# Attention with two exponential paths: VectorE's exp in half-step exponent bits, read through four shifted copies

## The chip, the core and the metric

The program runs on one NeuronCore of one Trainium2 chip. The metric is the time of one execution on the device in microseconds. The engines are TensorE (PE in the profile), VectorE (DVE), ScalarE (ACT), GpSimd (POOL) and SyncE (SP, which issues DMAs). PE writes into PSUM; ACT and DVE read PSUM; POOL works on SBUF alone.

## What is computed

One transformer block, conditioned by a vector c (adaptive layer norm), on 2048 tokens of width 512, in bfloat16:

```python
mod = (_silu(c) @ w_mod).reshape(c.shape[0], 6, 1, -1)
sa, ca, ga, sb, cb, gb = ...
h = _layernorm(x) * (1 + ca) + sa
qkv = (h @ wqkv)                        # 32 heads of 16
scores = einsum('bhqd,bhkd->bhqk', q, k) * 16 ** -0.5
o = einsum('bhqk,bhkd->bhqd', softmax(scores), v)
x = x + ga * (o @ wo)
h = _layernorm(x) * (1 + cb) + sb
x = x + gb * (gelu(h @ w1 + b1) @ w2 + b2)      # 512 -> 1376 -> 512
```

The bulk is the exponential: 32 heads x 2048 queries x 2048 keys.

## The kernel before

**Tiles.** Scores are computed transposed, with 128 keys on the partitions and 512 queries along the free dimension. The work is cut into 32 runs. A run handles one block of 512 queries for four heads at once (or, for the last block, 256 queries for eight heads) against 16 key tiles of 128 keys. A key tile of a run has four score blocks of 128x512, one for each of four row groups of PE. That makes 32 x 16 x 4 = 2048 score blocks. Each is one matmul at L852 (function `qk`), with the 16-wide heads selected by zeros in the masked q.

**Two paths to exp.** On path A the score blocks go in groups of three and two into PSUM tiles `st`, and ACT computes exp into `pt` (L925). On path D each block goes into a PSUM bank `ax`, and DVE computes exp by writing bits (L966): q is scaled so that a score is in 1/128 of a power of two, DVE adds a bias and writes int16, and these bits, read as bfloat16, are 2 to that power with a mantissa that is linear between powers of two. The error of the linear mantissa is averaged out: the same bits shifted by 26, 51, 77 and 102 (fifths of an octave, L987, 2048 columns at a time, into `sh`) are further copies, and each copy is multiplied with a copy of V that is scaled by the inverse power (`PH_W`), so that the five products add up to an exponential with a smaller ripple. The first copy is `ph` itself with the unscaled V (`VEB`); the others use `VX`. The last copy of some tiles is made by POOL in four pieces of 512 columns (`by_pool`, L1002, into `sg`).

**PV.** For each copy, four matmuls at L1037 (`pv_op`) add one key tile's product with V to the run's accumulator `od` in PSUM, whose 17th column for each head is the softmax denominator. A key tile of path A has one such PV group, a key tile of path D five. Tiles 2, 5, 8, 11 and 14 (`DKS`) of each run may take path D; ACT takes the ones that D has not reached when its own are finished (`next_tile`).

**The order of the work.** [...] A planner (`Plan`) has a list of ready operations for each engine with a duration, a priority, the buffers that they need and the time at which those come free. At each step it commits the operation that can start first; among those that can start within a short time of each other it takes the lowest value of priority plus a pseudorandom amount (`spread`, up to 0.15), which is drawn from a seed. `SEEDS` has 32 seeds, one for each 25 us of planned time. Matmuls of zeros into the running accumulator (`zeros`, L478 and L1028) and of a zero tile (`warm`, L462) are put into PE's pauses when the planner counts too little PE work in the last microseconds.

**Around the attention.** In the first 30 us the input is normalised, modulated and projected; POOL fills the copies `VX` (memsets at L583, scaling at L787). Denominators go out and back through DRAM (`normalise`). The output projection and the MLP of a finished query block (`block_tail`; L1204, L1270, L1210) run between the runs of the next one. After the last run only the last 256 queries' share remains (`last_half`; L1350, L1381, L1210).

**Buffers of path D.** `ph` has four buffers, `sh` three, `sg` one, all of 2048 int16 columns. A `ph` buffer comes free when all its readers are done: the PV group that reads it and the shifts.

Of the kernel before, what the change touches and what calls it, by code (L numbers as in the profile page):

```python
# [12 lines left out]
ALU = mybir.AluOpType  # L13
# [9 lines left out]

NPH = 5
PH_SH = [round(128 * j / NPH) for j in range(NPH)]


def _bf16(v):  # L30
    m, e = math.frexp(v)
    return math.ldexp(round(m * 256) / 256, e)


PH_W = [_bf16(2.0 ** (-sh / 128)) for sh in PH_SH]


def _gain():
    tot = 0.0
    for f in range(128):  # L40
        for sh, w in zip(PH_SH, PH_W):
            n, m = divmod(f + sh, 128)
            tot += w * 2.0 ** n * (1 + m / 128) / 2.0 ** (f / 128)
    return tot / 128


PH_B = 127.0 * 128.0 - 128.0 * math.log2(_gain())

# [10 lines left out]
FILL = 2.1  # L63
HOLD = 0.0
SPREAD = 0.15
SEEDS = (911, 176, 171, 436, 700, 513, 198, 752, 533, 913, 224, 342, 292, 722, 961, 407, 718, 35, 564, 862, 16, 658, 167, 214, 547, 531, 221, 674, 720, 595, 429, 662)
HEAT = 1.7


# [40 lines left out]
class Plan:  # L110
# [59 lines left out]
    def spread(self, o):  # L170
        x = ((sum(map(ord, o.kind)) if o.eng == "PE" else o.fn.__code__.co_firstlineno if o.fn else 0) * 2654435761 ^ SEEDS[min(int(self.now // 25.0), len(SEEDS) - 1)] * 2246822519) & 0xFFFFFFFF
        x = ((x ^ x >> 15) * 2246822519) & 0xFFFFFFFF
        return SPREAD * ((x ^ x >> 13) & 1023) / 1024.0
# [107 lines left out]
def kernel(  # L281
# [14 lines left out]
    nc = tc.nc  # L296
# [11 lines left out]
    FL = F - (NF - 1) * P  # L308
    VW = 17
    EPS = 1e-5  # L310
    QSC = 0.25 * 128.0 / math.log(2.0)
    ESC = math.log(2.0) / 128.0
    DKS = (2, 5, 8, 11, 14)
    NPT = 4
    FEW = 1
# [160 lines left out]
    def zeros(r):  # L476
        for i in range(4):
# [27 lines left out]
    VX = {(t, ph): keep.tile([P, 32 * VW + 15], BF16, name=f"VX{t}_{ph}")  # L505
          for t in DKS for ph in range(1, NPH)}
    kT = [[keep.tile([P, QB], BF16, name=f"kT{cc}_{b}") for b in range(NQ)] for cc in range(NC)]
# [26 lines left out]
    first = {}  # L534
# [53 lines left out]
    for b in range(NQ):  # L588
        late = (lambda: True) if b == 0 else (lambda: first_ln[0])
        o_v0[b] = v_init(VEB[b], PH_W[0], 1.0 + b, late)  # L590
        for t in DKS:
            if t // TPB == b:
                o_vx0[t] = [x for ph in range(1, NPH) for x in v_init(
                    VX[(t, ph)].unsqueeze(1), PH_W[ph], 1.5 + b, lambda: first_ln[0])]

# [172 lines left out]
    def make_v(b, cc, kind, acq, eng, after=None):  # L768
# [14 lines left out]
        for t in DKS:  # L783
            if t // TPB == b:
                def scale(o, t=t):
                    for ph in range(1, NPH):
                        nc.gpsimd.tensor_scalar(  # L787
                            out=v_cols(VX[(t, ph)])[:, 8 * cc:8 * cc + 8, 0:16],
                            in0=v_cols(v_tile(t, 0))[:, 8 * cc:8 * cc + 8, 0:16], scalar1=PH_W[ph],
                            scalar2=0.0, op0=ALU.mult, op1=ALU.add)  # L790
# [40 lines left out]
    def next_tile(which, r):  # L831
        while r < NR:
            if which == "A" and own[r]:
                return r, own[r].pop(0)
            if which == "A" and shared[r]:
                left[r] -= NPH - 1
                return r, shared[r].pop()
# [99 lines left out]
    def qk_d():  # L937
        r, kt, rows = at["D"]
        if not rows:
            got = next_tile("D", r)  # L940
            if got is None:
                return
            r, kt = got
            rows = [0, 1, 2, 3]
            at["D"][:] = r, kt, rows
            o_ph[0] = op("NIL", None, 0.0, (), lat=0.0, prio=0.0, acq=r_ph)
            d_e[:] = []
        ph = o_ph[0]
        live["D"] += 1
        deps, qm = qk_deps(r, kt)  # L950
        last = len(rows) == 1

        def go(o):
            n_d[0] += 1
            rows.remove(o.row)
            qk(o, 0, r, kt, o.row)
            live["D"] -= 1
        o = op("PE", go, MM, deps + [ph], lat=PEL, mode=("qk", rows[0]), kind="qkD", acq=r_ax, rel=(qm,),
               gate=lambda: n_d[0] - n_d[1] < 2)
        o.rows = rows  # L960

        def ex(e):
            n_d[1] += 1
            units[0] += 1
            d_last[0] = True
            nc.vector.tensor_scalar(out=ph.tile[:, o.row * QB:(o.row + 1) * QB], in0=o.tile, scalar1=PH_B,  # L966
                                    scalar2=0.0, op0=ALU.add, op1=ALU.max)
        d_e.append(op("DVE", ex, 0.6, (o,), lat=DL, prio=0.5, rel=(o,)))
        d_e[-1].run, d_e[-1].qk = r, o
        if last:  # L970
            shifts(r, kt, ph, list(d_e))
# [4 lines left out]
    def shifts(r, kt, first, es):  # L976
        def parts(o):
            return lambda: [o.tile[:, h * QB:(h + 1) * QB].bitcast(BF16) for h in range(4)]
        pv_op(r, kt, 0, es, parts(first), (first,))
        for j in range(1, NPH):  # L980
            if j == NPH - 1 and g_left[0] <= G_MAX and plan.now > G_FROM and (
                    r > a_run[0] or len(own[r]) + len(shared[r]) >= G_TILES):
                by_pool(r, kt, j, first, es, parts)
                continue
            def shift(o, j=j):
                d_last[0] = False
                nc.vector.tensor_scalar(out=o.tile, in0=first.tile, scalar1=PH_SH[j], scalar2=None, op0=ALU.add)  # L987
            sh = op("DVE", shift, 0.6, es, lat=DL, prio=2.0, acq=r_sh, rel=(first,), port=True)
            sh.run, sh.alt = r, True
            pv_op(r, kt, j, (sh,), parts(sh), (sh,))  # L990
# [4 lines left out]
    def by_pool(r, kt, j, first, es, parts):  # L995
        sh = op("NIL", None, 0.0, es[:1], lat=0.0, prio=0.0, acq=r_sg)
        got = []
        for h in range(4):
            def go(o, e=es[h]):
                g_left[0] -= 1  # L1000
                c = slice(e.qk.row * QB, (e.qk.row + 1) * QB)
                after_dve(nc.gpsimd.tensor_scalar(  # L1002
                    out=sh.tile[:, c], in0=first.tile[:, c], scalar1=1.0, scalar2=float(PH_SH[j]),
                    op0=ALU.mult, op1=ALU.add))
            g_left[0] += 1
            got.append(op("POOL", go, G_US, (sh, es[h]), lat=0.1, prio=G_PRIO, kind="beside", rel=(first,), port=True,
                          gate=lambda: plan.beside(G_MIN)))
        pv_op(r, kt, j, got, parts(sh), (sh,))

    def pv_op(r, kt, ph, deps, srcs, owners):  # L1010
        cc, par, hb = run_heads(r)

        def go(o):
            if not begun[r]:
                begun[r] = True
                pv_run[0] = r
                o_od[r] = o
                r_od.free[0] = 1e18
                o.acq, o.slot = r_od, 0
                o.tile = r_od.alloc(0)  # L1020
                first = True
            else:
                first = False
            left[r] -= 1
            got = srcs()
            if first and hb is not None:
                for i in range(4):
                    nc.tensor.matmul(out=o_od[r].tile[32 * i:32 * i + 32, :], lhsT=warm[:, 0:32],  # L1028
                                     rhs=warm[:, 0:1].to_broadcast([P, QB]), start=True,
                                     stop=False, tile_position=(0, 32 * i))  # L1030
            parts = (par,) if hb is None else (0, 1)
            for n, p in enumerate(parts):
                for i in range(4):
                    c0 = VW * (8 * cc + 2 * i + p)
                    w = QB if hb is None else HB
                    at = n * HB
                    nc.tensor.matmul(out=o_od[r].tile[32 * i:32 * i + 32, n * HB:n * HB + w],  # L1037
                                     lhsT=v_tile(kt, ph)[:, c0:c0 + 32],
                                     rhs=got[i][:, at:at + w], start=first and hb is None,
                                     stop=(left[r] == 0 and p == parts[-1]), tile_position=(0, 32 * i))  # L1040
            if o.extra:
                zeros(r)
            if left[r] == 0:
                o_last[r] = o
                ended.append(r)
        left[r] += 0

        def gate():
            return begun[r] or r_od.free[0] <= plan.now + 0.05 and (r == 0 or left[r - 1] == 0)
        o = Op("PE", go, 0.2225, list(deps) + o_v[(cc, kt // TPB)], lat=PEL, mode=("pv", 0), kind="pv",  # L1050
               rel=owners, gate=gate)
        o.last_left = lambda: left[r]
        plan.add(o)
# [396 lines left out]
    while True:  # L1450
# [7 lines left out]
        while ended:  # L1458
            r = ended.pop(0)
# [80 lines left out]
```

## Time and profile before

| | |
|---|---|
| time, three runs | 779.01 us median (778.93 to 780.66) |
| span of the profiled execution, first to last instruction | 777.3 us |
| PE busy | 736.9 us (95%) |
| DVE busy | 710.6 us (91%) |
| ACT busy | 750.7 us (97%) |
| POOL busy | 323.5 us (42%) |
| ACT's exp, L925 | 626 instructions, 709.7 us |
| DVE's exp, L966 | 484 instructions, 317.5 us |
| DVE's shifts, L987 | 406 instructions, 276.6 us |
| POOL's shift pieces, L1002 | 312 instructions, 191.3 us |

A row of a group gives line, engine, operation, output and inputs with shapes, then the count; behind the first bar the busy time in us (overlaps counted once in the page's groups) and the mean duration in ns; behind the second the idle time of the engine just before these instructions and what ended most of it. A row of a stretch gives its length, then for each engine busy time and the number of instructions, then the granted clock of PE, the share of time in which the DMA engines were busy, and GB/s. A row of the timeline or of the chain of waits gives start and duration in us. A PE that is busy isn't PE at its peak: matmuls overlap, and their ends are modelled.

### The profile page before, as it was taken

The numbers are of one execution on the slowest core, as the hardware profiler recorded it, in microseconds if no ns is written. First come the engines' busy times: TensorE is split into PE (matmuls) and PEld (weight loads), VectorE is DVE, ScalarE is ACT, GpSimd is POOL, SyncE is SP. The second block draws the span as 40 slices with busy tenths as digits, with TensorE's granted clock in tenths as the row PEclk, the third lists the DMA queues.
The fourth block names the chain that finished last, engine by engine and source line by source line (L and its number), as shares of the span: only waits on it lengthen the run. The fifth ranks groups of instructions, "written<-read, shape, count | busy, mean of one in ns | idle before, by whom it ended". The sixth has DMA issues, their size and how long they took to land.

```text
span 777.3 us, 21242 instructions
## 1 busy us (share of the span) xinstructions
PE 736.9 (95%) x8476; PEld 273.7 (35%) x8476; DVE 710.6 (91%) x1226; ACT 750.7 (97%) x677; POOL 323.5 (42%) x619
## 2 busy tenths in 40 slices
PE   8999999999998999999999999999999999999998
PEld 3433333233322222223323233233334444434455
DVE  6888699899999999999999899999899999998983
ACT  4999999999999999999999999999999999999993
POOL 6534645434445345545323144343334543252231
PEclk9999999999999999999999999999999999999999
DMA  7124010000210001001100100001020101010000
GB/s 217 35 76 143 19 40 28 26 12 12 76 26 23 19 18 50 19 7 27 40 20 21 35 19 26 12 21 33 29 56 22 25 19 45 16 26 18 26 18 28
DMA packets 38549, 27.74 MB, mean 36 GB/s; under 512 B 17941, under 2 KB 33846, under 8 KB 38450
## 3 DMA queue, kind: packets, MB, share of 16 engines
q1 hardware_dynamic: 38442, 26.39, 12.3%
q8 instruction: 66, 1.08, 0.6%
q14 instruction: 33, 0.27, 0.1%
q10 hardware_dynamic: 8, 0.00, 0.0%
HBM read 20.77 MB, written 2.61 MB: 30 GB/s over the span
## 4 chain that ended last, share of the span: by engine, by line
ACT 42%; PE 29%; DVE 15%; issue 11%; DMA 2%; POOL 0%; SPq 0%; DVEq 0%; ACTq 0%
ACT pt L925 41%; PE od L1037 9%; PE st L852 8%; DVE ph L966 5%; DVE sh L987 5%; PE ax L1210 3%; PE ax L852 2%; PE ax L1270 2%; PE ax L732 1%; DVE ln_s L637 1%; DVE OD L1062 1%; DMA blk<-in_w_mod_dram 1%; DMA dc<-dn 1%; PE ax L1204 1%; DVE z L648 1%
## 5 line engine op out<-in xcount | busy, mean ns | idle before, releaser
L925 ACT ACTIVATE pt<-st 128x1536 bf16<-128x1536 f32 x626 | 709.7, 1367 | 2.5 <-PE st L852 1.3
L966 DVE TENSOR_SCALAR ph<-ax 128x512 int16<-128x512 f32 x484 | 317.5, 681 | 26.9 <-PE ax L852 24.5
L1002 POOL TENSOR_SCALAR sg<-ph 128x512 int16<-128x512 int16 x312 | 191.3, 622 | 259.6 <-DVE sh L987 159.2
L987 DVE TENSOR_SCALAR sh<-ph 128x2048 int16<-128x2048 int16 x406 | 276.6, 709 | 4.9 <-PE od L1037 3.6
L852 PE MATMUL st<-qm,kT 32*128 32x512 bf16 x1564 | 245.2, 382 | 23.1 <-ACT pt L925 18.1
L852 PE MATMUL ax<-qm,kT 32*128 32x512 bf16 x484 | 166.6, 379 | 2.1 <-DVE ph L966 1.3
L852 PEld LDWEIGHTS <-kT 32*128 32x128 bf16 x2048 | 83.1, 91 | 239.1 <-issue 229.3
L1037 PE MATMUL od<-sh,VX 128*32 128x512 bf16 (+1 forms) x2036 | 144.1, 340 | 2.3 <-DVE sh L987 2.1
L1037 PE MATMUL od<-pt,VEB 128*32 128x512 bf16 (+1 forms) x1952 | 142.9, 340 | 0.9 <-DVE OD L1062 0.5
L1037 PEld LDWEIGHTS <-VEB 128*32 128x32 bf16 x2560 | 60.7, 96 | 74.2 <-issue 60.9
L1037 PEld LDWEIGHTS <-VX 128*32 128x32 bf16 x2432 | 57.7, 95 | 79.3 <-issue 68.3
L1089 POOL TENSOR_TENSOR OT<-OD,RB 128x256 bf16<-128x256 f32 x38 | 27.5, 736 | 64.7 <-DVE sh L987 57.7
L1037 PE MATMUL od<-ph,VEB 128*32 128x512 bf16 (+1 forms) x608 | 47.9, 340 | 1.2 <-DVE OD L1062 1.1
L1270 PE MATMUL ax<-blk,W 128*128 128x512 bf16 (+1 forms) x176 | 44.1, 356 | 0.1
L787 POOL TENSOR_SCALAR VX<-VEB 128x128 bf16<-128x128 bf16 x80 | 27.2, 342 | 31.5 <-DVE VEB L663 26.8
L732 PE MATMUL ax<-blk,w 128*128 128x512 bf16 x124 | 36.2, 383 | 1.3 <-DMA w<-in_A_wqkv_dram 0.8
L1210 PE MATMUL ax<-w,g 128*128 128x512 bf16 x128 | 33.7, 381 | 1.1 <-ACT g L1280 0.6
L1089 POOL TENSOR_TENSOR OS<-OD,RB 128x256 bf16<-128x256 f32 x24 | 17.5, 742 | 40.1 <-DVE sh L987 39.8
L1037 PE MATMUL od<-sg,VX 128*32 128x512 bf16 (+1 forms) x396 | 31.3, 339 | 0.0
L1275 DVE TENSOR_SCALAR g<-ax,b1c 128x512 bf16<-128x512 f32 (+1 forms) x44 | 29.3, 676 | 1.3 <-PE ax L1270 1.1
L478 PE MATMUL od<-warm 128*32 128x512 bf16 x268 | 26.0, 382 | 0.0
L637 DVE BATCH_NORM_STATS2 ln_s<-xb 128x6 f32<-128x512 bf16 x32 | 21.6, 675 | 1.5 <-DMA xb<-in_A_x_dram 1.4
(108 smaller groups left out, 409.6 us busy)
## 6 DMA issues: line engine op xcount, KB each, us to landing
RB<-rn SPq DMA_DIRECT2D x124, 64.0 KB
xb<-in_A_x_dram SPq DMA_DIRECT2D x7, 512.0 KB
out_dram<-o SPq DMA_DIRECT2D x16, 128.0 KB
qm<-qs SPq DMA_DIRECT2D x120, 16.0 KB
W<-in_B_w_dram SPq DMA_DIRECT2D x1, 1376.0 KB
w<-in_A_wqkv_dram SPq DMA_DIRECT2D x3, 384.0 KB
blk<-in_w_mod_dram SPq DMA_DIRECT2D x2, 512.0 KB
xb<-in_w_mod_dram SPq DMA_DIRECT2D x2, 512.0 KB
```

Of the source, the lines that this page charges most:

```text
L637: nc.vector.bn_stats(out=st6, in_=src)
L732: return chain([(lambda ps, j=j: nc.tensor.matmul(out=ps[:, 0:QB], lhsT=w.tile[:, j, cc * P:(cc + 1) * P], rhs=o_h[b].tile[:, j, :], start ...
L852: nc.tensor.matmul(out=o.tile[:, k * QB:(k + 1) * QB], lhsT=kT[cc][kb][rows, ko * P:(ko + 1) * P], rhs=qm.tile[rows, par, :] if hb is None ...
L925: nc.scalar.activation(out=e.tile[:, 0:total * QB], in_=o.tile[:, 0:total * QB], func=ACT.Exp, scale=ESC)
L966: nc.vector.tensor_scalar(out=ph.tile[:, o.row * QB:(o.row + 1) * QB], in0=o.tile, scalar1=PH_B, scalar2=0.0, op0=ALU.add, op1=ALU.max)
L987: nc.vector.tensor_scalar(out=o.tile, in0=first.tile, scalar1=PH_SH[j], scalar2=None, op0=ALU.add)
L1002: after_dve(nc.gpsimd.tensor_scalar(out=sh.tile[:, c], in0=first.tile[:, c], scalar1=1.0, scalar2=float(PH_SH[j]), op0=ALU.mult, op1=ALU.add))
L1037: nc.tensor.matmul(out=o_od[r].tile[32 * i:32 * i + 32, n * HB:n * HB + w], lhsT=v_tile(kt, ph)[:, c0:c0 + 32], rhs=got[i][:, at:at + w], ...
L1089: two = beside(lambda c: nc.gpsimd.tensor_tensor(out=OT.tile[:, c], in0=OD.tile[:, c], in1=o5.tile[:, c], op=ALU.mult), (OT,), (OD, o5), f ...
L1210: nc.tensor.matmul(out=ps, lhsT=g[:, f, col:col + P], rhs=rhs, start=(f == 0), stop=(f == NF - 1))
L1270: mm = chain([(lambda ps, f=f, j=j, f0=f0: nc.tensor.matmul(out=ps[:, (f - f0) * N:(f - f0 + 1) * N], lhsT=W1[:, j, f * P:(f + 1) * P], rh ...
L1275: ev.append(op("DVE", lambda o, f=f, f0=f0, mm=mm: nc.vector.tensor_scalar(out=g.tile[:, f, 0:N], in0=mm.tile[:, (f - f0) * N:(f - f0 + 1) ...
```

## The change

VectorE's exp writes its result in half steps: q is scaled by twice as much (`QSC` with `FINE` = 2), so the int16 counts 1/256 of an octave, and the exponent bias of 127 x 128 is no longer in it. These numbers aren't bfloat16 bits themselves, so the direct reading of `ph` is dropped. Four copies (0, 1/4, 1/2, 3/4 of an octave) are all made by an instruction with two operations: times 0.5, plus the bias, the shift and a fraction of 0.25 or 0.75, rounded when written as int16. The first copy goes with `VEB`, the other three with `VX`, of which there are now three for each of five tiles instead of four. ACT's exp has half the scale. The copy made by POOL is now the fourth one (j = 3), with a factor of 0.5 where 1.0 stood. The 32 seeds are other numbers. No other line differs; `Plan`, its durations and priorities, and the buffers are the same.

```diff
-NPH = 5
-PH_SH = [round(128 * j / NPH) for j in range(NPH)]
+NPH = 4
+FINE = 2
+PH_SH = [128 * j / NPH + 0.25 + 0.5 * (j % 2) for j in range(NPH)]
...
-PH_W = [_bf16(2.0 ** (-sh / 128)) for sh in PH_SH]
+PH_W = [_bf16(2.0 ** (-j / NPH)) for j in range(NPH)]
...
-PH_B = 127.0 * 128.0 - 128.0 * math.log2(_gain())
+PH_0 = 127.0 * 128.0
+PH_B = -FINE * 128.0 * math.log2(_gain())
+PH_LOW = -FINE * PH_0
...
-SEEDS = (911, 176, 171, 436, 700, 513, 198, 752, 533, 913, 224, 342, 292, 722, 961, 407, 718, 35, 564, 862, 16, 658, 167, 214, 547, 531, 221, 674, 720, 595, 429, 662)
+SEEDS = (133, 8, 244, 706, 635, 613, 830, 607, 557, 981, 249, 97, 553, 633, 53, 586, 376, 469, 873, 940, 563, 742, 976, 448, 82, 180, 131, 20, 555, 353, 321, 992)
...
-    QSC = 0.25 * 128.0 / math.log(2.0)
-    ESC = math.log(2.0) / 128.0
+    QSC = 0.25 * 128.0 * FINE / math.log(2.0)
+    ESC = math.log(2.0) / (128.0 * FINE)
...
             nc.vector.tensor_scalar(out=ph.tile[:, o.row * QB:(o.row + 1) * QB], in0=o.tile, scalar1=PH_B,
-                                    scalar2=0.0, op0=ALU.add, op1=ALU.max)
+                                    scalar2=PH_LOW, op0=ALU.add, op1=ALU.max)
...
-        pv_op(r, kt, 0, es, parts(first), (first,))
-        for j in range(1, NPH):
+        for j in range(NPH):
...
-                nc.vector.tensor_scalar(out=o.tile, in0=first.tile, scalar1=PH_SH[j], scalar2=None, op0=ALU.add)
+                nc.vector.tensor_scalar(out=o.tile, in0=first.tile, scalar1=1.0 / FINE, scalar2=PH_0 + PH_SH[j],
+                                        op0=ALU.mult, op1=ALU.add)
...
                 after_dve(nc.gpsimd.tensor_scalar(
-                    out=sh.tile[:, c], in0=first.tile[:, c], scalar1=1.0, scalar2=float(PH_SH[j]),
+                    out=sh.tile[:, c], in0=first.tile[:, c], scalar1=1.0 / FINE, scalar2=PH_0 + PH_SH[j],
                     op0=ALU.mult, op1=ALU.add))
```

`_gain` computes the mean of the summed copies over an octave, before in 128 steps and now in 256, with the rounding of the shifted value.

More of the change, by code (lines that the diff above doesn't have):

```diff
@@ L32, in _bf16 @@
     return math.ldexp(round(m * 256) / 256, e)
-PH_W = [_bf16(2.0 ** (-sh / 128)) for sh in PH_SH]
+PH_W = [_bf16(2.0 ** (-j / NPH)) for j in range(NPH)]
 def _gain():
     tot = 0.0
-    for f in range(128):
+    for f in range(128 * FINE):
         for sh, w in zip(PH_SH, PH_W):
-            n, m = divmod(f + sh, 128)
-            tot += w * 2.0 ** n * (1 + m / 128) / 2.0 ** (f / 128)
-    return tot / 128
-PH_B = 127.0 * 128.0 - 128.0 * math.log2(_gain())
+            n, m = divmod(round(f / FINE + sh), 128)
+            tot += w * 2.0 ** n * (1 + m / 128) / 2.0 ** (f / (128 * FINE))
+    return tot / (128 * FINE)
+PH_0 = 127.0 * 128.0
+PH_B = -FINE * 128.0 * math.log2(_gain())
+PH_LOW = -FINE * PH_0
 WIN = 3.4
```

## The prediction

> **What bounds the kernel now.** I read the cores view first, then busy time by stretches, then the groups of instructions and the waits of PE and DVE. The profiled span is 777.3 us; the three runs have a median of 779.01 us, so 1.7 us lie around the span, and I add the sum's differences to both alike.
>
> ```profile
> core 0: 777.3 us, clock 1.000
> 27.00:754.00 727.00, 694.87 (x8119) 251.51 (x8117) 681.43 (x1154) 725.24 (x633) 303.98 (x546) 1.00 0.12 31
> ```
>
> The columns behind the length are PE, PEld, DVE, ACT, POOL (busy us and instructions), granted clock, DMA share, GB/s. From 27 to 754 us, ScalarE (ACT) is busy for 725.24 of 727.00 us: it misses 1.76 us. VectorE (DVE) is idle for 45.57 us, PE for 32.13 us. In hundreds of microseconds:
>
> ```profile
> 100.00:200.00 100.00, 95.89 (x1072) 33.93 (x1071) 94.57 (x161) 100.00 (x90) 45.45 (x86) 1.00 0.10 26
> 200.00:300.00 100.00, 92.48 (x1035) 29.35 (x1031) 97.93 (x162) 99.69 (x89) 45.41 (x74) 1.00 0.13 35
> 300.00:400.00 100.00, 94.75 (x986) 29.82 (x983) 98.00 (x168) 99.36 (x89) 45.21 (x70) 1.00 0.10 24
> 400.00:500.00 100.00, 96.33 (x917) 30.59 (x909) 94.89 (x161) 99.94 (x85) 33.96 (x55) 1.00 0.08 22
> 500.00:600.00 100.00, 96.97 (x1144) 33.74 (x1140) 94.88 (x157) 99.80 (x86) 40.52 (x65) 1.00 0.12 31
> 600.00:700.00 100.00, 96.01 (x1464) 41.84 (x1464) 96.77 (x166) 99.47 (x86) 40.77 (x64) 1.00 0.10 26
> ```
>
> ACT never misses more than 0.64 us in a hundred (300 to 400), while DVE keeps 2.00 to 5.43 us free. Who waits for whom says the same:
>
> ```profile
> L925 ACT ACTIVATE pt<-st 128x1536 bf16<-128x1536 f32 x626 | 709.7, 1367 | 2.5 <-PE st L852 1.3
> L852 PE MATMUL st<-qm,kT 32*128 32x512 bf16 x1564 | 245.2, 382 | 23.1 <-ACT pt L925 18.1
> L966 DVE TENSOR_SCALAR ph<-ax 128x512 int16<-128x512 f32 x484 | 317.5, 681 | 26.9 <-PE ax L852 24.5
> L987 DVE TENSOR_SCALAR sh<-ph 128x2048 int16<-128x2048 int16 x406 | 276.6, 709 | 4.9 <-PE od L1037 3.6
> ```
>
> PE stands 18.1 us waiting for ACT to free a score bank; ACT stands 1.3 us waiting for PE. So ACT sets the end, and DVE comes a close second. A score block is one 512-wide matmul: 1564 go to ACT and 484 to DVE, 2048 in all. One block costs ACT 709.7/1564 = 0.454 us.
>
> **The change part by part.** Counts of the changed kernel are of its instructions as built.
>
> *Division of blocks.* The hand-written order gives 1556 blocks to ACT and 492 to DVE: two key tiles move, 123 instead of 121. ACT loses 8 x 0.454 = 3.63 us. DVE gains 8 exp at 317.5/484 = 0.656 and 4 shifts (410 instead of 406) at 276.6/406 = 0.681, together 8.0 us; GpSimd's shift pieces go from 312 to 328. DVE's cover is the 45.57 us of idle time, 5.7 times the need; per hundred it is 1.1 us against at least 2.00. Without that cover all 8.0 us would come later, less ACT's 3.6.
>
> *The price of a shift.* A shift had one operation (add), now it has two (multiply, add); exp keeps two. Rows that bear on a second operation:
>
> ```profile
> L1275 DVE TENSOR_SCALAR g<-ax,b1c 128x512 bf16<-128x512 f32 x33 | 24.5, 743 | 1.3 <-PE ax L1270 1.1
> L754 DVE TENSOR_SCALAR qs<-ax 128x512 bf16<-128x512 f32 x15 | 10.3, 683 | 0.5 <-PE ax L732 0.4
> L1275 DVE TENSOR_SCALAR g<-ax,b1c 128x256 bf16<-128x256 f32 x11 | 4.8, 474 | 0.0
> L648 DVE TENSOR_SCALAR z<-xb,mv,rs x32: 381/404/592, 6.9 to 762.9; 128x512 bf16<-128x512 bf16 x32
> L987 DVE TENSOR_SCALAR sh<-ph x406: 622/683/1172, 44.5 to 750.5; 128x2048 int16<-128x2048 int16 x136
> ```
>
> Over the same 512 float32 elements, qs with one operation takes 683 ns, and exp (ph) with two takes 681: the second is free there. For 16-bit SBUF data the only two-operation row is z, of another shape, so I take it apart. From g, 256 elements more cost 743 - 474 = 269 ns, 1.05 ns each. Then exp's fixed part is 681 - 512 x 1.05 = 143 ns, and g's 205: a per-partition operand costs 62. A shift of 2048 elements takes 683 in the median; at four elements per 1.05 ns that is 538 + 145, the same fixed part. z has two per-partition operands: 404 - 145 - 2 x 62 = 135 ns for 512 elements, and four per step would be 134. So z, with two operations on 16-bit data, runs at the shifts' rate. I take 0 ns more. Bounds: -2 ns (exp against qs) and +62 ns (the largest addition that any operand shows); beyond them a lost rate, below. On GpSimd the shift was multiply and add already and keeps its form: 0.
>
> *The direct reading goes.* A key tile was read by five PV groups, now by four, all from shifted copies: 121 x 5 = 605 groups become 123 x 4 = 492, and ACT's two tiles fewer need 2 fewer, 115 in all. A group of four matmuls follows the one ahead of it by 0.22 us:
>
> ```profile
> 409.42 0.40 PE L1037 MATMUL od<-ph,VEB 128*32 128x512 bf16 x4
> 409.64 0.39 PE L1037 MATMUL od<-sh,VX 128*32 128x512 bf16 x4
> ```
>
> That takes 25.3 us off PE; zero matmuls, which keep PE busy, go from 300 to 464:
>
> ```profile
> L478 PE MATMUL od<-warm 128*32 128x512 bf16 x268 | 26.0, 382 | 0.0
> L1028 PE MATMUL od<-warm 128*32 128x512 bf16 x32 | 3.2, 389 | 0.2 <-DVE OD L1062 0.2
> PE od L1037 <- DVE sh L987: 2.1, 7, 0.5
> ```
>
> These 41 groups put 9.0 us back, so PE is 16 us lighter. PE isn't what ACT waits for, so this is worth nothing by itself; at best it removes ACT's missing 1.76 us, at worst nothing. I take 0. The direct PV needed only the four exps; now the first PV also needs a shift. What is queued behind it on PE is the next score matmul, on which ACT waits; PE stood 2.1 us in 7 waits on a shift before (last row). If these doubled, PE's 18.1 us of waiting for ACT cover it: 0, bound +2.1.
>
> *V copies and the start.* Three scaled copies of V for each of five key tiles replace four: 20 of 80 VX scalings and 15 of 60 memsets leave POOL. One lies on the chain of the start:
>
> ```profile
> 17.93 1.46 POOL L787 TENSOR_SCALAR VX<-VEB 128x128 bf16<-128x128 bf16 x4
> 19.78 0.71 POOL L644 TENSOR_TENSOR rs<-rs,mhalf 128x2 f32<-128x2 f32 x1
> 22.33 1.44 ACT L653 ACTIVATE blk<-ax,modA 128x512 bf16<-128x512 bf16 x2 [0.42 <-PE ax L690]
> ```
>
> The second pair of rs waits behind four scalings of 1.46/4 = 0.365 us each, and z, transposes and ACT's modulation (0.42 us idle) follow it. Three scalings are 0.365 us less: I take -0.3 us (bounds -0.365 and 0). SP and its DMAs are the same in number and kind.
>
> *The end.* New seeds reorder the last stage:
>
> ```profile
> 752.59 0.38 PE L852 MATMUL st<-qm,kT 32*128 32x512 bf16 x1
> 754.93 0.45 DVE L1336 STREAM_TRANSPOSE OD<-od 128x256 f32<-128x256 f32 x1 [3.42 <-PE od L1037]
> 756.14 0.42 DVE L1343 TENSOR_TENSOR OT<-od,OD 128x256 bf16<-128x256 f32 x1
> ...
> 753.99 1.28 ACT L1280
> 755.29 0.64 ACT g L1280
> 755.97 0.61 PE ax L1210 x2
> 757.87 0.43 PE t L1350 x2
> 769.22 4.55 PE ax L1210 x21
> ```
>
> The lower rows are the chain: table load and gelu on ACT, then PE. A full-wide matmul takes 0.43/2 = 0.215 us there, a half-wide one half of it. Behind the last score matmul stood three PV or zero groups and three full-wide warming matmuls, 3 x 0.22 + 3 x 0.215 = 1.3 us; now 12 half-wide W1 matmuls and five groups stand there, 12 x 0.108 + 5 x 0.22 = 2.4 us. So the last PV ends near 752.59 + 0.38 + 2.4 = 755.4, and DVE's transposes start 0.4 us later than at 754.93. The last heads' output projection (L1350) waits for OT, ready at 756.56, but PE comes to it at 757.87 after gelu's matmuls: 1.3 us cover the 0.4. The second row tile is projected later than the first by more matmuls than before, but its way through DVE runs under the first one's 44 W1 matmuls. I take 0, bounds -0.6 and +0.6.
>
> *Sum.* -3.63 (ACT) + 0 (DVE's extra work and second operation) + 0 (PE) - 0.3 (start) + 0 (end) = -3.9 us: a span of 773.4 and a time of 779.0 - 3.9 = 775.1 us. The bounds that need no failure: -3.63 - 0.365 - 1.76 - 0.6 = -6.4 (772.7), and -3.63 + 2.1 + 0.6 = -0.9 (778.1).
>
> **The rivals.** *ACT goes hungry by the new order.* Which matmul stands where between two exps is drawn anew by the seeds. If every hundred microseconds were as bad as 300 to 400 (0.64 us missing), ACT would miss 7.27 x 0.64 = 4.7 us in place of 1.76: 775.1 + 2.9 = 778.0, no measurable change. For it: DVE has less spare time, so its lateness reaches PE sooner. Against it: PE has 16 us less to do, and already waits far more for ACT than ACT for PE.
>
> *DVE becomes the pacer; the result is slower.* Place: the shift, L987, through the PV behind it to the next score matmul. At +62 ns DVE gets 410 x 0.062 = 25.4 us and the 8.0 us, 4.6 us per hundred. Against the idle times 5.4, 2.1, 2.0, 5.1, 5.1 and 3.2, this is short by 2.5 + 2.6 + 1.4 = 6.5 us if all idle time can be used, by 16 us if half of it can; the middle, 11 us, gives 775.1 + 11 = 786. With half of it usable, the shortage exceeds the whole gain from about 25 ns a shift on. Against it: exp's two operations and z's fixed part. A far version, where integer data with a multiplication goes at half the rate (z is bfloat16), costs 538 ns a shift, 220 us on DVE, less some 35 us of idle time: about 960 us. No row shows that form, so I leave it a few per cent.
>
> *PE's clock drops.* The clock was 1.00 in every stretch, with zero matmuls filling PE's pauses. With real PE work down by 25 us, that filling may not suffice everywhere. One stretch of 25 us at half clock doubles PE's work there; PE is busy for 694.87 of 727 us, of which 75 groups of zeros (16.5 us) are filling, so up to 25 x (2 x 678/727 - 1) = 22 us, and nothing where busy time is mostly waiting inside the array: middle 11 us, 786 us. The Trainium skill, "TensorE: Matmul & The Clock Gate", section "What's actually happening", says that the array's default state is throttled and that recent activity, judged in windows of some 3.4 us, releases it; by that rule a lighter PE can be slower. The trace of before agrees only in that a busy PE kept 1.00; no run here shows a drop.
>
> *The split doesn't do what it says:* ACT's exps take longer when DVE and PE are rearranged, and the gain is nil; this has the same time as the hungry ACT, and goes with it.
>
> **How the numbers follow.** A measurement of this kernel can tell 0.3% (2.3 us) from no change: faster is below 776.7, slower above 781.3. The forecast (ACT's eight blocks, with small gains or losses) has 0.62, of which 0.06 lies in its upper edge, above 776.7. The hungry ACT has 0.20: 0.16 no change, 0.01 faster, 0.03 worse than 781.3. DVE as pacer has 0.13, the half rate in it, all of it slower; the clock 0.05, of which 0.01 is a drop too short to tell. So faster is 0.57, same 0.23, slower 0.20. The range starts below the best bound of 772.7, with the spread of single runs (778.93 to 780.66 before) in mind, at 772.0, and goes to 784.0, which takes in the hungry ACT and the mild half of the slower cases and leaves out the rest, some 0.12. The forecast's own range is 772.7 to 778.1.
>
> **What would show it.** 623 ACTIVATEs at L926 in place of 626 with 706 us in sum, and ACT missing about 1.8 us between 27 us and its last exp: right. L987 at a median near 683 ns and DVE idle near 38 us in the same stretch: the price of the second operation is right; a median above 710 speaks for DVE as pacer, above 1100 for the half rate. PE waiting 18 us or more for ACT, granted clock 1.00 throughout: PE is no bound. rs about 0.4 us earlier near 19 us: the start. The forecast is wrong if ACT misses over 6 us, wherever that comes from, or if the stage after the last exp (23.3 us of span from 753.99 on) grows by over a microsecond.

## The result and the profile after

The changed kernel takes 776.38 us in the median of five runs (775.06 to 777.12), the kernel before 779.30 us in five (778.93 to 780.66). The ratio is 0.9954 with a 95% interval of 0.9941 to 0.9967: faster by 0.46%, give or take 0.13%. The profiled execution took 775.14 us with a span of 773.3 us, which is 4.0 us less than the span of before.

Columns are those explained before. Of the changed kernel, first the busy time in the stretch from 27 us to the end of ACT's last exp:

```profile
27.00:750.36 723.36, 675.15 (x7608) 241.61 (x7677) 688.56 (x1163) 721.43 (x630) 309.56 (x526) 1.00 0.11 31
```

Then the page's groups of exps:

```profile
L926 ACT ACTIVATE pt<-st 128x1536 bf16<-128x1536 f32 x623 | 705.9, 1358 | 2.8 <-PE st L853 1.0
L967 DVE TENSOR_SCALAR ph<-ax 128x512 int16<-128x512 f32 x492 | 322.5, 681 | 26.8 <-PE ax L853 24.9
```

The view of the shifts' line, with minimum, median and maximum in ns:

```profile
L987 DVE TENSOR_SCALAR sh<-ph x410: 623/683/1208, 44.5 to 749.7; 128x2048 int16<-128x2048 int16 x137
```

And the longest of PE's waits (total us, times, longest):

```profile
PE st L853 <- ACT pt L926: 24.1, 87, 0.6
```

ACT's exps take 705.9 us instead of 709.7, and it misses 723.36 - 721.43 = 1.9 us in this stretch (1.76 before). The median shift is still 683 ns. PE waits 24.1 us for ACT, 6 more than before. DVE's idle time shrank from 45.6 to 34.8 us.

The timeline of ACT shows where the 4.0 us lie; the rows are the first and the last exps and what follows them, of the kernel before and of the changed one:

```profile
15.03 6.89 ACT L925 ACTIVATE pt<-st 128x1536 bf16<-128x1536 f32 x6 [0.49 <-PE st L852]
753.99 1.28 ACT L1280 ACT_TABLE_LOAD   x1
```

```profile
14.66 6.88 ACT L926 ACTIVATE pt<-st 128x1536 bf16<-128x1536 f32 x6 [0.49 <-PE st L853]
750.36 1.28 ACT L1281 ACT_TABLE_LOAD   x1
```

The start is 0.37 us shorter, the stretch from the first exp to the end of the last is 735.70 us instead of 738.96 (-3.26), and what follows to the end of the span is 22.9 instead of 23.3 us (-0.37). So most of the gain lies in ACT's stretch, as large as the saved exps (-3.8) less half a microsecond of other lateness.

### The profile page after: what moved, and what is told of

Same layout as the page of the kernel before. It is cut to its first block, busy times and chain, and to the rows that moved or that the text cites. A ratio compares the mean times of both kernels' runs of the same rounds, so it can differ in the third digit from the quotient of the medians.

```text
span 773.3 us, 20346 instructions
## 1 busy us (share of the span) xinstructions
PE 717.4 (93%) x7984; PEld 264.3 (34%) x8060; DVE 719.7 (93%) x1238; ACT 747.3 (97%) x674; POOL 329.3 (43%) x600
## 3 DMA queue, kind: packets, MB, share of 16 engines
q8 instruction: 63, 1.03, 0.5%
## 4 chain that ended last, share of the span: by engine, by line
ACT 46%; PE 28%; issue 13%; DVE 11%; POOL 1%; DMA 0%; SPq 0%; DVEq 0%; POOLq 0%; ACTq 0%
ACT pt L926 45%; PE od L1038 8%; PE st L853 8%; DVE ph L967 4%; PE ax L1211 3%; DVE sh L987 3%; PE ax L853 2%; PE ax L733 1%; PE od L479 1%; PE ax L1271 1%; DVE ln_s L638 1%; PE ax L463 1%; DVE OD L1063 1%; DVE z L649 1%; PE t L1382 1%
## 5 line engine op out<-in xcount | busy, mean ns | idle before, releaser
L926 ACT ACTIVATE pt<-st 128x1536 bf16<-128x1536 f32 x623 | 705.9, 1358 | 2.8 <-PE st L853 1.0
L967 DVE TENSOR_SCALAR ph<-ax 128x512 int16<-128x512 f32 x492 | 322.5, 681 | 26.8 <-PE ax L853 24.9
L1003 POOL TENSOR_SCALAR sg<-ph 128x512 int16<-128x512 int16 x328 | 205.0, 625 | 305.7 <-DVE sh L987 197.9
L987 DVE TENSOR_SCALAR sh<-ph 128x2048 int16<-128x2048 int16 x410 | 280.4, 713 | 2.0 <-PE od L1038 1.0
L853 PE MATMUL st<-qm,kT 32*128 32x512 bf16 x1556 | 243.7, 382 | 32.3 <-ACT pt L926 24.1
L1038 PE MATMUL od<-sh,VX 128*32 128x512 bf16 (+1 forms) x1428 | 106.5, 342 | 2.1 <-DVE sh L987 1.9
L1038 PEld LDWEIGHTS <-VX 128*32 128x32 bf16 x1848 | 44.4, 95 | 71.0 <-issue 63.8
L1038 PE MATMUL od<-sh,VEB 128*32 128x512 bf16 (+1 forms) x616 | 48.6, 340 | 2.3 <-DVE OD L1063 2.1
L479 PE MATMUL od<-warm 128*32 128x512 bf16 x432 | 41.6, 382 | 0.0
L733 PE MATMUL ax<-blk,w 128*128 128x512 bf16 x100 | 32.2, 382 | 2.5 <-issue 0.6
L788 POOL TENSOR_SCALAR VX<-VEB 128x128 bf16<-128x128 bf16 x60 | 20.8, 348 | 20.7 <-DVE VEB L664 17.3
```

The lines of the kernel that those rows point to most:

```text
L733: return chain([(lambda ps, j=j: nc.tensor.matmul(out=ps[:, 0:QB], lhsT=w.tile[:, j, cc * P:(cc + 1) * P], rhs=o_h[b].tile[:, j, :], start ...
L853: nc.tensor.matmul(out=o.tile[:, k * QB:(k + 1) * QB], lhsT=kT[cc][kb][rows, ko * P:(ko + 1) * P], rhs=qm.tile[rows, par, :] if hb is None ...
L926: nc.scalar.activation(out=e.tile[:, 0:total * QB], in_=o.tile[:, 0:total * QB], func=ACT.Exp, scale=ESC)
L1003: after_dve(nc.gpsimd.tensor_scalar(out=sh.tile[:, c], in0=first.tile[:, c], scalar1=1.0 / FINE, scalar2=PH_0 + PH_SH[j], op0=ALU.mult, op ...
```

## The experiments

Each ran beside the kernel before on the same chip; behind a measured time stand, in brackets, its ratio to that kernel and the 95% interval of the ratio. Differences to the changed kernel are taken from its 776.38 us above, which were measured apart from these runs; the kernel before had medians of 779.20 to 779.63 us beside the experiments and 779.30 us there. In what follows, ACT's stretch is the time from the start of its first exp to the end of the last, and the end is the rest of the span after it; both are read from ACT's timeline as above.

### Is it the number of ACT's blocks, or the four copies, or the list of seeds?

Seeds alone change how many key tiles DVE gets. This was counted in the programs as built; only the lists shown below were run. Of 40 lists drawn at random, the changed kernel has 118 to 122 tiles with a mean of 119.9; the kernel before, in the 35 of these lists that give it a complete order, has 118 to 123 with a mean of 119.9. So four copies as such bring DVE no tile; the 123 belong to the chosen list. The first run takes one of these lists with 123 tiles on the old formula, the second one with 118 on the new.

```diff
-SEEDS = (911, 176, 171, 436, 700, 513, 198, 752, 533, 913, 224, 342, 292, 722, 961, 407, 718, 35, 564, 862, 16, 658, 167, 214, 547, 531, 221, 674, 720, 595, 429, 662)
+SEEDS = (809, 286, 483, 265, 198, 709, 619, 979, 352, 457, 827, 959, 740, 357, 977, 997, 373, 82, 225, 104, 232, 481, 201, 345, 209, 494, 639, 921, 624, 860, 1, 490)
```

> The kernel before with its five copies and direct reading, and another list of 32 seeds with which DVE gets 123 key tiles as in the changed kernel (492 exps of DVE, 1556 blocks for ACT, 412 shifts on DVE). Theory A (the gain is the number of ACT's blocks, whoever brings it, and PE's relief is worth nothing): 8 x 0.454 = 3.6 us under the kernel before, near 775.7, ACT missing about 2 us between 27 us and its last exp. Theory B (the lighter PE of the four copies carries the gain: with five copies PE can't feed ACT when DVE does 123 tiles): ACT misses 4 us or more, 778 us or above.

```diff
-SEEDS = (133, 8, 244, 706, 635, 613, 830, 607, 557, 981, 249, 97, 553, 633, 53, 586, 376, 469, 873, 940, 563, 742, 976, 448, 82, 180, 131, 20, 555, 353, 321, 992)
+SEEDS = (767, 956, 142, 444, 892, 199, 845, 894, 216, 28, 257, 217, 299, 513, 246, 782, 600, 333, 265, 557, 429, 854, 134, 62, 931, 757, 362, 919, 469, 678, 597, 834)
```

> The changed kernel with another list of seeds with which DVE gets only 118 key tiles (472 exps of DVE, 1576 blocks for ACT). Theory A: 12 blocks more on ACT than in the kernel before, 12 x 0.454 = 5.4 us over it, near 784.5. Theory B: the lighter PE keeps part of the gain, under 782.

Measured: 794.9 us (1.0202, 1.0189 to 1.0215) and 796.0 us (1.0215, 1.0201 to 1.0228). Theory A misses both by 11 us or more. Theory B's letter takes in the first (778 us or above, ACT missing over 4 us) but not the second, where four copies were to stay under 782. The group of exps on the page of the five copies with 123 tiles:

```profile
L925 ACT ACTIVATE pt<-st 128x1536 bf16<-128x1536 f32 x623 | 705.9, 1360 | 9.1 <-PE od L1037 5.6
```

And ACT's timeline of that run:

```profile
18.52 6.88 ACT L925 ACTIVATE pt<-st 128x1536 bf16<-128x1536 f32 x6 [0.49 <-PE st L852]
766.17 1.28 ACT L1280 ACT_TABLE_LOAD   x1 [6.33 <-DVE g L1275]
```

The eight blocks are saved to the digit: 705.9 us, as in the changed kernel. But the first exp comes 3.5 us later, ACT is idle 9.1 us before exps instead of 2.5, and after the last exp (its end is 766.17 - 6.33 = 759.84) the table load waits 6.33 us for DVE's evictions of the W1 results, so the end takes 32.9 us instead of 23.3. The order decides these three, not the number of blocks. With 118 tiles it is the same: exps of 715.0 us, the first at 17.8, an end of 26.1 us, and 7.3 us idle before exps; so ACT goes hungry with four copies too, and a fifth copy isn't the cause that theory B takes it for. Theory A sized its own term right and left out all the rest that a list of seeds sets.

To get that term alone, the next kernel keeps the changed kernel's order until DVE has begun 121 tiles.

```diff
-    turn = [0]
+    turn = [0, 0]
...
-            if which == "D" and shared[r] and r >= d_run():
-                return r, shared[r].pop(0)
+            if which == "D" and shared[r] and r >= d_run() and turn[1] < 121:
+                turn[1] += 1; return r, shared[r].pop(0)
```

> The changed kernel with the same order up to the point where DVE has begun 121 key tiles; the last tiles go to ACT (1564 blocks). Theory A: the changed kernel's time plus 3.6 us, near 779.5, ACT's exp at 709.5 us. Theory B: under 778.

Measured: 780.51 us (12 runs, 778.81 to 782.11; 1.0009, 0.9999 to 1.0020), 4.1 us over the changed kernel where 3.6 were expected. Its exps take 709.5 us, 3.6 more. Theory A holds within the order: take the two tiles away and the gain is gone, so that at equal blocks the time can't be told from the kernel before.

The next two leave the seeds out altogether, in each of the two kernels:

```diff
-SPREAD = 0.15
+SPREAD = 0.0
```

> The changed kernel with the pseudorandom part of the planner's choice set to 0, so the planner's bare order: 120 key tiles on DVE. Theory S (the lists of seeds, chosen for each kernel, carry nearly all): over 783, its start, its end and ACT's waits each some us worse than with the chosen list. Theory F (four copies are better by themselves): 779 or below.

> The kernel before with the pseudorandom part set to 0: 119 key tiles on DVE. Theory S: over 785, and over the four copies without seeds by their 4 blocks (1.8 us) give or take 3 us for the order. Theory F: over the four copies without seeds by 5 us or more.

Measured: 790.19 us (1.0149, 1.0123 to 1.0175) for four copies and 793.06 us (1.0171, 1.0150 to 1.0191) for five. Each kernel's chosen list is worth some 14 us against its bare order. The difference of 2.9 us between the two has overlapping intervals, and the four blocks account for 1.8 of it by the price of a block (1.4 by the exps of the two profiles, 711.6 and 713.0 us); theory S holds.

The last pair has one random list in both kernels, with 121 tiles in both:

```diff
+SEEDS = (530, 543, 568, 494, 803, 795, 108, 904, 573, 58, 254, 195, 283, 43, 790, 100, 519, 463, 575, 28, 778, 915, 934, 64, 453, 333, 627, 996, 517, 620, 524, 204)
```

> The changed kernel with a list of seeds drawn at random, the same list as in the five-copy run beside it; both have 121 key tiles on DVE, so ACT has 1564 blocks in both. Theory S (the list makes the order, and the order the time): 785 to 797, and either of the two kernels may be the faster one. Theory F (four copies are better by themselves, by PE's relief): at least 2 us below the five copies with this list.

> The kernel before with the same random list of seeds, 121 key tiles on DVE as with its own list. Theory S: 785 to 797 although ACT's share is that of the 779 us kernel; the difference lies in the start, in ACT's waits and in the stage after the last exp. Theory F: at least 2 us above the four copies with this list.

Measured: 785.30 us (1.0080, 1.0063 to 1.0097) with four copies, 790.56 us (1.0148, 1.0131 to 1.0165) with five. Theory F's bound of 2 us is met, 5.3 us for four copies. But ACT's timeline puts it elsewhere than PE's relief; first the kernel with four copies, then the one with five:

```profile
752.87 2.86 ACT L926 ACTIVATE pt<-st 128x1024 bf16<-128x1024 f32 x3 [0.35 <-PE st L853]
755.74 1.28 ACT L1281 ACT_TABLE_LOAD   x1
762.98 2.12 ACT L1281 ACTIVATE g<-g 128x2304 bf16<-128x2304 bf16 x1 [5.32 <-DVE g L1276]
```

```profile
747.79 8.72 ACT L925 ACTIVATE pt<-st 128x1536 bf16<-128x1536 f32 x8 [0.51 <-PE ax L852]
767.24 1.28 ACT L1280 ACT_TABLE_LOAD   x1 [10.73 <-DVE g L1275]
```

The last exp ends at 755.7 with four copies and at 767.24 - 10.73 = 756.5 with five; both began at about 14.5. So through the whole attention, with equal blocks, the lighter PE is worth under a microsecond in this pair. Even that may be the clock: in the five-copy profile it fell to 0.93 from 275 to 300 us and from 700 to 725 us, where ACT misses 1.2 and 1.4 us. Behind it, the five-copy order has put the W1 evictions so late that ACT waits 10.73 us, and the spans end at 783.8 and 790.6. Whether four copies make such ends rarer can't be said from one pair.

### What the second operation costs, and DVE as pacer

The kernel before with its own order, its shift written as two operations:

```diff
-                nc.vector.tensor_scalar(out=o.tile, in0=first.tile, scalar1=PH_SH[j], scalar2=None, op0=ALU.add)
+                nc.vector.tensor_scalar(out=o.tile, in0=first.tile, scalar1=1.0, scalar2=float(PH_SH[j]), op0=ALU.mult, op1=ALU.add)
```

> The kernel before, in its own order, with its shift on DVE as two operations (times 1.0, plus the shift). Theory A (the second operation is free): the median of the 406 shifts stays at 683 ns within 5, time as before. Rival (an operation more costs up to 62 ns): a median of 745 and ACT missing more.

Measured, in the view of that line (minimum, median, maximum in ns):

```profile
L987 DVE TENSOR_SCALAR sh<-ph x406: 623/685/1175, 44.3 to 752.0; 128x2048 int16<-128x2048 int16 x136
```

685 against 683 ns: the second operation is free on int16 too, within 2 ns. The one run took 780.71 us, within the range of the kernel before on that chip (778.26 to 781.26).

Now the rival's price, put on the changed kernel by a column for the factor:

```diff
-    warm = const.tile([P, P], BF16, name="warm")
-    o_warm = op("POOL", lambda o: nc.gpsimd.memset(warm, 0.0), 0.2, prio=-1.0)
+    warm, half_c = const.tile([P, P], BF16, name="warm"), const.tile([P, 1], FP32, name="half_c")
+    o_warm = op("POOL", lambda o: (nc.gpsimd.memset(warm, 0.0), nc.gpsimd.memset(half_c, 1.0 / FINE)), 0.2, prio=-1.0)
...
-                nc.vector.tensor_scalar(out=o.tile, in0=first.tile, scalar1=1.0 / FINE, scalar2=PH_0 + PH_SH[j],
+                nc.vector.tensor_scalar(out=o.tile, in0=first.tile, scalar1=half_c, scalar2=PH_0 + PH_SH[j],
```

> The changed kernel in its own order with the factor 0.5 of DVE's shift read from a per-partition column instead of an immediate. This prices DVE as pacer: the median shift rises by 62 ns to 745, 25 us more of DVE work. Theory A (idle time of DVE can be used by half): 776.4 + 11 = 787, between 782 and 792 as the prediction has it. Rival (DVE has slack enough in the order): under 779.

Measured: 785.22 us (1.0069, 1.0049 to 1.0089), 8.8 us over the changed kernel: within theory A's range, under its middle of 787, and far from the rival's 779. The view of the line, then the group of exps, then PE's waits:

```profile
L987 DVE TENSOR_SCALAR sh<-ph,half_c x410: 653/742/1211, 45.1 to 760.3; 128x2048 int16<-128x2048 int16 x137
```

```profile
L926 ACT ACTIVATE pt<-st 128x1536 bf16<-128x1536 f32 x623 | 709.9, 1292 | 8.3 <-PE st L853 4.5 <-PE ax L853 1.9 <-PE od L1038 0.6
```

```profile
PE ax L853 <- DVE ph L967: 7.6, 25, 0.9
PE od L1038 <- DVE sh L987: 3.9, 14, 0.6
```

A median shift 59 ns longer is 24 us of DVE work, and a good third of it reaches the end. The way is the one that the prediction's rival, DVE as pacer, named: PE's waits for DVE, 2.4 and 2.1 us in the changed kernel, are 7.6 and 3.9, and the score matmuls behind them come late to ACT.

### What PE's load is worth

The changed kernel in its own order with a group of zero matmuls behind each DVE tile's first PV group, so that PE carries what the fifth copy cost:

```diff
-            pv_op(r, kt, j, (sh,), parts(sh), (sh,))
+            pv_op(r, kt, j, (sh,), parts(sh), (sh,), j == 0)
...
-    def pv_op(r, kt, ph, deps, srcs, owners):
+    def pv_op(r, kt, ph, deps, srcs, owners, fifth=False):
...
-            if o.extra:
-                zeros(r)
+            if o.extra or fifth and left[r] > 0:
+                [zeros(r) for _ in range(o.extra + (fifth and left[r] > 0))]
```

> The changed kernel in its own order; behind the first PV group of each of DVE's key tiles stands one more group of four zero matmuls into the same accumulator (123 groups less those at a run's end, 27 us of PE work), so PE has the load of five copies with the rest untouched. Theory A (PE's relief is worth nothing by itself): within 1 us of the changed kernel, near 776.4; PE's waiting for ACT falls from 24 us. Theory B (the relief is what lets ACT run on): ACT misses 3 us or more on top, 779 or above.

Measured: 782.87 us (1.0042, 1.0027 to 1.0056), 6.5 us over the changed kernel: theory A is wrong here, and theory B's time holds. The group of exps, and PE's wait:

```profile
L926 ACT ACTIVATE pt<-st 128x1536 bf16<-128x1536 f32 x623 | 710.3, 1281 | 5.5 <-PE ax L853 2.0 <-PE st L853 1.3 <-PE od L1038 0.6
```

```profile
PE st L853 <- ACT pt L926: 17.0, 60, 0.7
```

The same 623 exps take 710.3 us instead of 705.9, and idle time before them doubles to 5.5. Only 7 us of the 27 come out of PE's waiting for ACT (24.1 to 17.0). The reading that fits, not shown by itself, is that PE's waits lie in the pauses that ACT leaves it, and a group put where there is no pause delays the next score block by its own length.

The opposite edit takes the filling away, in the changed kernel's own order:

```diff
 def zeros(r):
-        for i in range(4):
+        for i in range(0):
```

> The changed kernel in its own order without the 108 groups of zero matmuls that fill PE's pauses between score blocks (those that clear an accumulator stay). Theory C (the clock rival: filling is what keeps the clock at 1.00): the granted clock falls below 0.97 in the mean and the time goes over 782. Rival (the filling is PE load without use): clock 1.00 and, as each added group of the fifth-group run cost 6.5/123 = 0.053 us, up to 108 x 0.053 = 5.7 us less than the changed kernel, near 771.

Measured: 781.91 us (11 runs, 780.28 to 784.45; 1.0035, 1.0023 to 1.0047), 5.5 us over the changed kernel, with a mean granted clock of 0.975 to 0.985. The rival's 771 us is refuted. Theory C was right that the filling holds the clock; its two numbers, a clock below 0.97 and a time over 782, were both just missed. Two stretches of that run:

```profile
250.00:275.00 25.00, 21.71 (x207) 6.28 (x202) 24.06 (x41) 24.46 (x23) 12.89 (x20) 0.93 0.08 22
625.00:650.00 25.00, 23.02 (x303) 9.35 (x304) 22.87 (x41) 23.00 (x21) 10.82 (x17) 0.86 0.08 19
```

Where the clock column falls, ACT misses 0.5 and 2.0 us. Of the 25 stretches from 100 to 725 us, 18 are at 1.00, and in those ACT misses at most 0.16 us each, 0.4 us together; in the changed kernel, with its filling, it misses 0.5 us in the same 18. So the groups that the planner put into pauses cost ACT nothing, unlike the 123 put in afterwards.

With the filling in place there are lapses too. The run with 121 tiles has one, in 5 us of its profile (columns as before, clock third from the end):

```profile
125.00:130.00 5.00, 5.00 (x56) 1.42 (x55) 3.58 (x6) 3.51 (x4) 1.06 (x2) 0.67 0.19 54
130.00:135.00 5.00, 5.00 (x50) 1.35 (x46) 4.70 (x8) 5.00 (x5) 2.63 (x4) 1.00 0.00 2
```

ACT loses 1.5 us there. The single runs of both kernels go the same way, though the ranges of the second overlap: the two runs of the changed kernel with a mean clock of 1.000 took 775.06 and 775.14 us, the three with 0.997 or 0.998 took 776.38 to 777.12. The kernel before, beside the run without filling, took 778.32 to 779.87 us at 1.000 and 779.22 to 781.71 below it.

## Why the prediction was right, and where not

**ACT's eight blocks** (-3.63): right. The exps fell by 3.8 us, the stretch by 3.26, and the cap at 121 tiles gives 4.1 us back.

**DVE's extra 8.0 us and the second operation at 0 ns**: right. The median shift is 683 ns, 685 with two operations in the old order, and DVE took its extra work (7.1 us busier) out of its idle time (45.6 to 34.8 us; the 38 us that the prediction named left out that the stretch would be 3.6 us shorter). The first PV's new wait for a shift, with a bound of +2.1, cost nothing: PE waits 2.1 us in 7 waits on shifts, as before.

**PE's relief at 0**: the value was right for this change, the reason only in part. The prediction said that PE isn't what ACT waits for and that its 18.1 us of waiting are cover. The run with the fifth group shows that 27 us more of PE work in a finished order cost 6.5 us. The pair with one list and equal blocks shows under 1 us between four and five copies through the attention. Both fit together if an order that is made with a PE load places it in the pauses. For the filling, the run without it shows this; for the PV groups it is argued.

**The start at -0.3**: the step failed, and the term is 0. The three scalings took 1.03 us instead of 1.46, and the second pair of z began at 19.80 us instead of 20.52. But ACT's modulation, which the prediction lets wait for them, came 7.31 us after the first exp, as before (22.33 - 15.03 = 7.30 us). The last transposes in front of it stand at the end of a row of PE work without a pause, which begins when an exp frees a score bank; of the changed kernel, two rows of PE and one of ACT:

```profile
19.34 0.39 PE L853 MATMUL st<-qm,kT 32*128 32x512 bf16 x2 [0.20 <-ACT pt L926]
21.31 0.62 PE L691 MATMUL ax<-ident,z 128*128 128x128 bf16 x8
21.97 1.45 ACT L654 ACTIVATE blk<-ax,modA 128x512 bf16<-128x512 bf16 x2 [0.42 <-PE ax L691]
```

In the kernel before the first two stand at 19.70 and 21.67 us, as far apart. ACT's fourth key copy began at 39.68 us, as before (39.65). The 0.37 us by which the start is shorter lie before the first exp, and so before the scalings; that start varies between runs: 14.1 us in the run without filling, 15.23 with 121 tiles, 14.66 in the changed kernel.

**The end at 0**: right within its bounds (-0.37). The longer PE queue behind the last score matmul was covered; the transposes of the last run began 1.9 us after the last exp's end, while L1351 came 3.9 us after it, as L1350 did before. The delay itself was mis-sized: the prediction set the new end of the PV (755.4) against the old start of the transposes and got 0.4 us, and it is 1.0 us (the transposes began 0.9 us after the last exp before). That left little of the 1.3 us of cover.

**The rivals.** The hungry ACT didn't come with the chosen list. With other lists or none, ACT was idle before its exps for 3.5 to 9.3 us (2.5 before), and the ends took up to 34 us. The prediction priced it at 2.9 us from one stretch of a kernel that has a chosen list; the runs with other lists or none took 6 to 17 us more than the kernel before, and much of it lies outside that term: with 123 tiles and five copies 3.5 us in the start and 9.6 in the end, of 15.4 us of span. Part of the hunger also goes with the clock. Here is one stretch of the run with 118 tiles, then of the four copies without seeds, where ACT misses 4.3 and 5.5 us, beside 7.3 and 9.3 us of idle time before all exps:

```profile
600.00:700.00 100.00, 93.14 (x1370) 38.99 (x1367) 92.19 (x158) 95.68 (x85) 40.72 (x62) 0.97 0.09 24
600.00:700.00 100.00, 91.11 (x1271) 37.80 (x1282) 88.85 (x151) 94.53 (x80) 35.26 (x54) 0.95 0.09 23
```

Whether the order's waits brought the clock down there, or the clock made the waits, no run tells.

DVE as pacer was priced at 11 us between 6.5 and 16, and costs 8.8. The clock rival had the right mechanism and too high a price: the lapse in the run with 121 tiles lasts under 5 us and costs 1.5 us, not 11 in a stretch of 25; its full form without filling costs 5.5. The change itself didn't make lapses more frequent as far as the runs show: 3 of its 5 runs have a mean clock below 1.000, and so have 11 of 16 of the kernel before beside the run without filling.

**The forecast as a whole.** 775.1 us was the sum for an execution at full clock, as the profile of before was, and such executions took 775.06 and 775.14. That it fits to a tenth is in part luck: ACT's stretch gave 3.26 us of the 3.63, and the 0.37 us each from the start and the end didn't come by the terms that the prediction had for them. The median run is 1.3 us longer at a mean clock of 0.997; that a lapse makes the difference is argued from the clocks, as no profile of such a run was taken.

What stays open is how much of the gain the four copies bring by themselves. The lists of seeds move the time by more than the gain in either direction, and each kernel has its own list; what is shown is that the formula together with its list gains 0.46%.

## What to carry to other kernels

Where an order is drawn by lot and then selected, an edit can't be judged by keeping the old list or by one new one: count what the order gives to the engine that sets the end (here blocks for ACT, 0.454 us each), then look at the start, the end and the waits, which a fresh list changes by more. A busy engine isn't a full one: compare the busy time of equal work (705.9 and 710.3 us for the same 623 exps, while the mean duration of one fell from 1358 to 1281 ns: they overlapped less), since late starts of overlapping instructions show up as busy time. And an engine that waits for the bottleneck has room only at the places where it waits.

## What was unexpected

A per-partition column in place of an immediate costs 59 ns on each DVE shift of 2048 int16 elements (742 against 683 ns), about what the float32 row of another operation had suggested (62 ns). Zero matmuls, which compute nothing, are worth 5.5 us: without 108 groups of them the granted clock fell to 0.975 to 0.985 in the mean. The Trainium skill, "TensorE: Matmul & The Clock Gate", section "What's actually happening", describes a clock that recent activity holds open, and the run without filling agrees: the same useful work, less activity, a lower clock.
